# Masked scores set to one value in the heads by queries, no mean of v put in, POOL and two-input DVE work planned as one resource, identity products in PE's gaps

## The chip, the cores and the metric

The kernel runs on one core of one Trainium2 chip. Its engines work side by side, each through its own list of instructions in order: TensorE (PE, with its weight loads PEld), VectorE (DVE), ScalarE (ACT), GpSimd (POOL) and SyncE (SP, which only issues transfers). The metric is the device time of one execution in microseconds: the median of three is 716.46 (716.38 to 717.63).

## The reference

Two parts follow each other: attention in which a query sees only the keys of its own hash bucket, then an MLP with a gate that mixes over the sequence.

```python
batch, n_heads, seq, head_dim = (4, 8, 768, 64)      # proj: (64, 6); d_model 512, d_ff 1024
def _attn_ref(q, k, v, proj):
    scale = 1.0 / np.sqrt(D)
    q_bits = (np.einsum('bhsd,dk->bhsk', q, proj) > 0).astype(np.int64)
    k_bits = (np.einsum('bhsd,dk->bhsk', k, proj) > 0).astype(np.int64)
    q_bucket = np.sum(q_bits * powers, axis=-1)
    k_bucket = np.sum(k_bits * powers, axis=-1)
    mask = q_bucket[:, :, :, None] == k_bucket[:, :, None, :]
    scores = scale * np.matmul(q, k.transpose(0, 1, 3, 2))
    scores = np.where(mask, scores, -1000000000.0)
    scores = scores - np.max(scores, axis=-1, keepdims=True)
    attn = np.exp(scores)
    attn = attn / (np.sum(attn, axis=-1, keepdims=True) + 1e-09)
    return np.matmul(attn, v).astype(np.float32)
def _moe_ref(x, w_in, w_spatial, b_spatial, w_out):
    h = np.maximum(x @ w_in, 0.0)
    u, v = (h[..., :d_ff // 2], h[..., d_ff // 2:])
    v_n = (v - mean(v)) / np.sqrt(var(v) + 1e-06)
    v_s = np.einsum('ts,bsd->btd', w_spatial, v_n) + b_spatial[None, :, None]
    return ((u * v_s) @ w_out).astype(np.float32)
```

A query whose bucket holds no key has all its scores at the same value after the mask. Its softmax is even over the 768 keys, and its output is the mean of v over the sequence.

## The kernel before, in words

**Tiles and loops.** The 32 heads of the four batches are taken two at a time: 16 pairs, four to a batch. A pair is worked through in 6 steps of 128 rows, so there are 96 steps. Numbers are kept to about the precision of float32 by splitting each one into two float16 parts, a high one and the rest; hence the many operations named `high` and `low`, and the three products for each product of the reference.

**The mask.** `hash_rows` takes the signs of the projections, and writes them by DMA (L367) as extra rows beside the rows of q and k. One more product over these rows adds a large negative number to every score whose buckets differ, larger with each bit in which they differ. So masked scores are far below the others, yet not all alike.

**Heads by queries and heads by keys.** Most heads are worked by queries (`by_queries`): a tile has 128 queries by 768 keys. DVE reads the scores from PSUM, scales them and takes the minimum of their negatives along the row (L486, which writes `ex` and the row's number into `nb`); ACT makes the exponential with `nb` as its bias (L489) and the high half (L493); DVE or POOL makes the rest (L497); SP issues a transposing DMA, `pt` from `pp` (L501); and PE multiplies by v (`weighted`, L607). The heads in the set `WIDE`, 2, 4 and 6, are worked by keys (`by_keys`): a tile has 128 keys by 768 queries, in float32, with no transpose. Their row maximum must be known beforehand: `row_max` computes the scores another time on PE, DVE reduces them (L554), and `max_row` turns the result and moves it by DMA (L581) into one of the mask's rows. All scores of the pair wait for that row.

**The mean of v.** A row without a key has masked scores that differ among themselves, so its softmax isn't even. For each pair `mean_v` (POOL, L417, L421, L424) and `mean_row` (PE L437, ACT L441) compute the mean of v. For each head `normalize` multiplies the result of such rows by zero (the third small DVE operation of `factor`, L632), makes a tile with the mean in these rows and zero elsewhere (`none`, POOL, L624 and L625) and adds it (`add`, POOL, L639; DVE for the last head). Then come the split of x (ACT L646, DVE L649) and its transpose.

**The MLP of a batch** is cut into units of PE work (`v_unit`, `u_unit`, `s_unit`, `o_unit`; PE line L702 for all). Their rank comes after that of the scores, so they fill what PE leaves free in the attention of the next batch. `norm` has the layer norm: statistics on DVE, the inverse root by ACT and a small Newton step, scaling on DVE (L834), the high part on ACT (L839), the rest on POOL (L843). In `s_unit` two products of 128x384 (L903, L906) are on POOL, in the last batch on DVE or POOL. The weights come as 64-bit or 32-bit numbers, and 24 of the 36 jobs in `weights` are converted by four DVE instructions (L287 to L292), two or three of ACT and one of POOL (L303).

**What sets the order.** A planner, run when the program is built. Every operation is an `Op` with its engine (or two to choose from, as "VG" for DVE or POOL), an assumed duration, what it depends on, the buffers it holds, and a rank. `timetable` plays the engines forward: the engine that can start first takes the ready operation of the lowest rank; PSUM banks of two pools, `m` and `pv`, are counted. The sequence of planned starts is then each engine's real order. At run time only the data dependences hold an engine back; the planned times themselves don't. The scores of step g are not planned before a time that grows by `T_FIRST`, `T_KEYS`, `T_QUERIES` or `T_LAST` a step, and the weights' jobs not before `W_FROM - 6 + W_EVERY * i`. DVE and POOL are planned as though they never met.

## Time and profile before

| | us |
|---|---|
| median of 3 executions | 716.46 (716.38 to 717.63) |
| the profiled execution | 722.25, its span 720.5 |
| PE busy | 632.9 (88%), mean granted clock 0.94 |
| DVE busy | 550.1 (76%) |
| ACT busy | 463.1 (64%) |
| POOL busy | 427.0 (59%) |
| transposing DMAs `pt` from `pp` | 174 |
| heads by queries, by keys | 29, 3 |

The span is the time from the first to the last instruction of the one profiled execution, which is a little longer than the others. A group's row gives its busy time, the mean length of one instruction in ns, and after the bar the idle time of the engine just before these instructions, with what ended it. The length of an instruction includes time in which it has been started and can't go on. The chain of waits is followed back from the last instruction: at each step to what released it.

### The profile page before, as it was taken

The numbers are of one execution on the slowest core, as the hardware profiler recorded it, in microseconds if no ns is written. First come the engines' busy times: TensorE is split into PE (matmuls) and PEld (weight loads), VectorE is DVE, ScalarE is ACT, GpSimd is POOL, SyncE is SP. The second block draws the span as 40 slices with busy tenths as digits, with TensorE's granted clock in tenths as the row PEclk, the third lists the DMA queues.
The fourth block names the chain that finished last, engine by engine and source line by source line (L and its number), as shares of the span: only waits on it lengthen the run. The fifth ranks groups of instructions, "written<-read, shape, count | busy, mean of one in ns | idle before, by whom it ended". The sixth has DMA issues, their size and how long they took to land.

```text
span 720.5 us, 16877 instructions
## 1 busy us (share of the span) xinstructions
PE 632.9 (88%) x6667; PEld 371.5 (52%) x6667; DVE 550.1 (76%) x1004; ACT 463.1 (64%) x707; POOL 427.0 (59%) x456
## 2 busy tenths in 40 slices
PE   3778989876887899789999899879899999989997
PEld 1344757643544555446544565445454556545553
DVE  6997977979799989687878997967879794273250
ACT  2956665978786777667686677666677784443112
POOL 6581853688556788967857686856867545025000
PEclk9876988988999999899999899989999999999999
DMA  5896876699999699999999799899788998000102
GB/s 184 183 216 137 137 173 145 132 200 203 198 209 187 116 185 186 220 190 226 185 179 203 140 172 211 165 158 199 158 162 133 210 136 137 0 15 30 45 1 87
DMA packets 318259, 110.84 MB, mean 154 GB/s; under 512 B 305124, under 2 KB 308196, under 8 KB 318180
## 3 DMA queue, kind: packets, MB, share of 16 engines
q1 hardware_dynamic: 314244, 108.62, 77.4%
q0 software_dynamic: 3840, 1.12, 1.0%
q8 instruction: 52, 0.85, 0.5%
q14 instruction: 27, 0.22, 0.1%
q10 hardware_dynamic: 96, 0.04, 0.0%
HBM read 27.94 MB, written 6.29 MB: 48 GB/s over the span
## 4 chain that ended last, share of the span: by engine, by line
PE 35%; DVE 28%; DMA 13%; ACT 11%; issue 9%; POOL 2%; SPq 0%; DVEq 0%; ACTq 0%; POOLq 0%
DMA pt<-pp 10%; DVE ex L486 9%; PE sps L702 8%; PE sp L459 7%; PE ops L702 6%; PE pv L607 6%; DVE pp L497 5%; ACT pp L493 4%; ACT ex L489 3%; DVE hl L385 3%; PE ups L702 3%; PE vpp L702 2%; PE mx L459 2%; DVE vr L834 1%; DVE bs L791 1%
## 5 line engine op out<-in xcount | busy, mean ns | idle before, releaser
L489 ACT ACTIVATE ex<-ex,nb 128x768 f32<-128x768 f32 x174 | 157.9, 933 | 94.7 <-DVE ex L486 94.6
L497 POOL TENSOR_TENSOR pp<-ex,pp 128x768 f16<-128x768 f32 x76 | 136.1, 1792 | 93.2 <-ACT pp L493 85.5
L486 DVE TENSOR_SCALAR_CACHE_REDUCE ex<-sp 128x768 f32<-128x768 f32 x174 | 160.0, 949 | 22.0 <-PE sp L459 21.9
L497 DVE TENSOR_TENSOR pp<-ex,pp 128x768 f16<-128x768 f32 x98 | 123.8, 1266 | 44.8 <-ACT pp L493 43.3
L607 PEld LDWEIGHTS <-pt 128*128 128x128 f16 x3132 | 116.5, 100 | 61.4 <-issue 34.3
L459 PE MATMUL sp<-hl 64*128 64x384 f16 x1080 | 124.5, 351 | 25.4 <-DVE ex L486 23.8
L493 ACT CAST pp<-ex 128x768 f16<-128x768 f32 x174 | 138.5, 822 | 7.2 <-DMA pt<-pp 6.6
L607 PE MATMUL pv<-vp,pt 128*128 128x65 f16 (+1 forms) x3132 | 128.5, 197 | 16.5 <-DVE x L636 9.2
L702 PE MATMUL sps<-ws,vn 128*128 128x384 f16 x576 | 101.1, 326 | 2.1 <-ACT vr L785 2.0
L459 PEld LDWEIGHTS <-hl 64*128 64x128 f16 x1104 | 56.8, 100 | 88.6 <-issue 64.2
L702 PEld LDWEIGHTS <-vn 128*128 128x128 f16 x576 | 53.8, 98 | 36.6 <-issue 3.8
L702 PE MATMUL ops<-wo,g 128*128 128x512 f16 x288 | 67.5, 382 | 3.2 <-DVE u L865 3.2
L702 PE MATMUL ups<-xt,wi 128*128 128x384 f16 x348 | 66.2, 334 | 2.9 <-DVE sg L352 2.8
L367 POOL DMA_DIRECT2D hk<-sg x112 | 59.5, 537 | 14.7 <-PE pv L607 6.8
L459 PE MATMUL sp<-hk 63*128 63x384 f16 (+1 forms) x360 | 54.7, 348 | 8.4 <-DMA hk<-sg 5.9
L702 PE MATMUL vps<-wi,xt 128*128 128x512 f16 x234 | 56.5, 379 | 1.7 <-ACT vr L785 1.2
L903 POOL TENSOR_TENSOR sy<-sy,u 128x384 f32<-128x384 f32 x24 | 27.2, 1134 | 49.3 <-DVE sy L891 48.9
L702 PEld LDWEIGHTS <-wi 128*128 128x128 f16 x384 | 35.8, 100 | 27.2 <-issue 6.2
L891 DVE SCALAR_TENSOR_TENSOR sy<-sps,bt 128x384 f32<-128x384 f32 x32 | 17.7, 552 | 36.2 <-PE sps L702 36.1
L702 PEld LDWEIGHTS <-g 128*128 128x128 f16 x288 | 26.7, 98 | 34.1 <-issue 5.8
L639 POOL TENSOR_TENSOR x<-x,xf 128x384 f32<-128x384 f32 x31 | 34.6, 1115 | 11.1 <-DVE x L636 8.7
L702 PEld LDWEIGHTS <-xt 128*128 128x128 f16 x288 | 25.9, 97 | 29.1 <-issue 3.7
(111 smaller groups left out, 845.7 us busy)
## 6 DMA issues: line engine op xcount, KB each, us to landing
qk<-kq SPq DMA_DIRECT2D x16, 768.0 KB
out<-o SPq DMA_DIRECT2D x24, 256.0 KB
v<-v SPq DMA_DIRECT2D x13, 384.0 KB
pt<-pp SPq DMA_TRANSPOSE x174
raw<-w_in SPq DMA_DIRECT2D x8, 256.0 KB
raws<-w_in SPq DMA_DIRECT2D x8, 256.0 KB
hk<-sg POOLq DMA_DIRECT2D x112, 9.0 KB, 3.5
vf<-v SPq DMA_DIRECT2D x3, 384.0 KB
```

Source lines behind the costliest of these rows:

```text
L367: eng.dma_start(out=hkt(p)[D * e:D * e + 2 * NB, 1 - j // 2, (j % 2) * HS:(j % 2 + 1) * HS], in_=sg[1][32 * j + 16 * e:32 * j + 16 * e + 2 ...
L385: op("V", 0.9, lambda to=to, part=part, frm=frm: nc.vector.scalar_tensor_tensor(out=st["hl", p][:, to], in0=st["qk", p][:, part], scalar=S ...
L459: nc.tensor.matmul(ps[e][:, c - halves[0]], lhsT=src[r, l, rows], rhs=src[r, m, cs], start=(a == 0), stop=(a == len(passes) - 1))
L486: nc.vector.tensor_scalar(ex, st["sc", p, i][e], -ISQ, None, op0=ALU.mult, op1=ALU.min, accum_out=st["nb", n][:, i:i + 1])
L489: nc.scalar.activation(st["e32", n, i], st["e32", n, i], AF.Exp, bias=st["nb", n][:, i:i + 1], scale=-1.0)
L493: nc.scalar.copy(st["pp", n, i][:, 0], st["e32", n, i])
L497: eng.tensor_tensor(out=st["pp", n, i][:, 1], in0=st.pop(("e32", n, i)), in1=st["pp", n, i][:, 0], op=ALU.subtract)
L607: nc.tensor.matmul(o, lhsT=l, rhs=m, start=(i == 0 and k == 0), stop=(i == NT - 1 and k == len(todo_) - 1))
L639: eng.tensor_add(st["x", n], st["x", n], st["f"])
L702: nc.tensor.matmul(c[0], lhsT=l(), rhs=r(), start=(j == 0), stop=(j == len(products) - 1))
L891: nc.vector.scalar_tensor_tensor(out=y[0], in0=c[0], scalar=1.0 / (SN * SW), in1=bt[:, hs], op0=ALU.mult, op1=ALU.add)
L903: t1 = op(*POST[last], lambda: either(t1).tensor_mul(y[0], y[0], u[h][:, d]), t, done["u", d, h], on=[hy, hu[h]], rank=2)
```

## The change

In heads by queries the DVE pass over the scores becomes a maximum with -2^28, a number between the real and the masked scores: all masked scores of a tile take that one value, and the row's maximum comes out beside them. A new small operation, `bias`, on ACT or POOL by the plan, multiplies the maximum by a constant for the exponential's bias, and the exponential has the scale. A row without a key has then 768 equal scores. So these heads need no mean of v, no `none`, no `add` and no third operation in `factor`; the heads by keys still do.

Head 2 goes from the heads by keys to the heads by queries. The planner marks the operations of POOL (but not its DMA issues, nor `bias`) and most of DVE's operations with two SBUF inputs or of the small `tensor_scalar` kind as `alone`: one of them is not planned before the one before it has ended. Several assumed durations are changed to go with it. The layer norm's scaling moves from DVE to ACT, with one more small DVE operation for its bias. The two products in `s_unit` may be on DVE in every batch, and the `low` of `normalize` on POOL. Wherever the plan has PE idle for over 0.5 us after its first 5 us and a bank of `m` is free, `warm` puts products of the identity with itself there, one for each 0.08 us. The steps of heads by queries are planned 6.0 us apart, not 5.8, and the weights' jobs 2.6 us apart, not 3.6.

```diff
-    WIDE = {2, 4, 6}
+    WIDE = {4, 6}
 def op(..., alone=False):
+        o.need, o.gives, o.alone = need, gives, alone or "G" in e and fn.__name__ not in ("move", "bias")
 timetable:
+        port = [0.0]
+        fill = []
             if not o.need:
-                return o.ready
+                return max(o.ready, port[0]) if o.alone else o.ready
...
+            gap = t - free[e]
+            if e == "P" and gap > GAP and free[e] > WARM and banks["m"] and min(banks["m"]) < free[e]:
+                fill.append((free[e], int((gap - 0.1) / 0.08)))
...
+            if o.alone:
+                port[0] = end
...
+        for t, n in fill:
+            op("P", 0.0, lambda n=n: warm(n)).start = t
+
+    def warm(n):
+        b = bank_m("warm")
+        for _ in range(n):
+            nc.tensor.matmul(b[:, :P], lhsT=ident, rhs=ident, start=True, stop=True)
 mean_v, mean_row:
+        if not keys(p):
+            return
 by_queries:
-            nc.vector.tensor_scalar(ex, st["sc", p, i][e], -ISQ, None, op0=ALU.mult, op1=ALU.min, accum_out=st["nb", n][:, i:i + 1])
+            nc.vector.tensor_scalar(ex, st["sc", p, i][e], -float(2 ** 28), None, op0=ALU.max, op1=ALU.max, accum_out=st["mx", n][:, i:i + 1])
+        def bias():
+            nb, mx = st["nb", n][:, i:i + 1], st["mx", n][:, i:i + 1]
+            if t1.e == "G":
+                nc.gpsimd.tensor_scalar(nb, mx, -ISQ, None, op0=ALU.mult)
+            else:
+                nc.scalar.activation(nb, mx, AF.Copy, scale=-ISQ)
-            nc.scalar.activation(st["e32", n, i], st["e32", n, i], AF.Exp, bias=st["nb", n][:, i:i + 1], scale=-1.0)
+            nc.scalar.activation(st["e32", n, i], st["e32", n, i], AF.Exp, bias=st["nb", n][:, i:i + 1], scale=ISQ)
...
-        t = t3 = op("VG", (1.1, 1.75), rest, t, on=[hx, hp], rank=(g, 1 + e))
+        at["nb", n] = t = t1 = op("AG", BIAS, bias, t, on=[held["nb", n], held["mr", n]], rank=(g, 0.1 + 0.1 * e))
+        t = t3 = op("VG", REST, rest, t, on=[hx, hp], rank=(g, 1 + e))
 normalize:
-            nc.vector.scalar_tensor_tensor(out=rv, in0=st["nb", n], scalar=ISQ * 2 ** 28, in1=rv, op0=ALU.is_le, op1=ALU.mult)
+            if n in KEYS:
+                nc.vector.scalar_tensor_tensor(out=rv, in0=st["nb", n], scalar=ISQ * 2 ** 28, in1=rv, op0=ALU.is_le, op1=ALU.mult)
-        at["xs", n] = op("V", 0.5, low, t, on=[hx, hs], rank=(g, 0.8))
+        at["xs", n] = op("VG", (0.55, 1.0), low, t, on=[hx, hs], rank=(g, 0.8))
 s_unit, norm:
-    POST = {False: ("G", 1.15), True: ("VG", (0.5, 1.15))}
+    POST = ("VG", (0.56, 1.0))
+                nc.vector.scalar_tensor_tensor(out=ve, in0=mv[g][:, :, 0], scalar=-1.0, in1=r, op0=ALU.mult, op1=ALU.mult)
-                    nc.vector.tensor_scalar(v32[i], v32[i], mv[g][:, j, 0:1], c["r"][:, j:j + 1], op0=ALU.subtract, op1=ALU.mult)
+                    nc.scalar.activation(v32[i], v32[i], AF.Identity, bias=c["ve"][:, j:j + 1], scale=c["r"][:, j:j + 1])
 constants:
-    T_FIRST, T_KEYS, T_QUERIES, T_LAST = 5.0, 4.8, 5.8, 5.8
+    T_FIRST, T_KEYS, T_QUERIES, T_LAST = 5.0, 4.8, 6.0, 6.0
+    REST, BIAS = (0.96, 1.68), (0.25, 0.25)
+    GAP, WARM = 0.5, 5.0
-    W_FROM, W_EVERY = 20.0, 3.6
+    W_FROM, W_EVERY = 20.0, 2.6
```

More of the change, by code (lines that the diff above doesn't have):

```diff
@@ L82, in __init__ @@
             self.left, self.then, self.ready, self.start = 0, [], 0.0, None
-            self.need, self.gives = None, None
+            self.need, self.gives, self.alone = None, None, None
             ops.append(self)
@@ L101, in __init__, with op @@
             self.users, self.before, self.closed = [], [], False
-    def op(e, d, fn, *after, on=(), rank=4, land=0.0, dma=0.0, need=None, gives=None):
+    def op(e, d, fn, *after, on=(), rank=4, land=0.0, dma=0.0, need=None, gives=None, alone=False):
         o = Op(e, d, fn, rank, land, dma)
-        o.need, o.gives = need, gives
+        o.need, o.gives, o.alone = need, gives, alone or "G" in e and fn.__name__ not in ("move", "bias")
         wait = [a for a in after if a is not None]
@@ L211, in lsh_attention_spatial_gating @@
     nc.sync.dma_start(out=hc, in_=hconst)
+    make_identity(nc, ident)
     ws = [const.tile([P, NT, S], F16, name=f"ws{i}") for i in range(2)]
@@ L232, in lsh_attention_spatial_gating @@
     nc.gpsimd.memset(ones, 1.0)
-    make_identity(nc, ident)
     wi = [const.tile([P, NPAIR, DF], F16, name=f"wi{i}") for i in range(2)]
@@ L407, in split_v @@
         t = op("A", 0.15 + 0.6 * z, high, at["v", p], *after, on=[held["v", p], h], rank=(NT * p - 1, 4))
-        at["vp", p] = op("V", 0.1 + 0.8 * z, low, t, on=[held["v", p], h], rank=(NT * p - 1, 4))
+        at["vp", p] = op("V", 0.1 + 0.8 * z, low, t, on=[held["v", p], h], rank=(NT * p - 1, 4), alone=True)
     def mean_v(p, *after):
+        if not keys(p):
+            return
         va, vc = buf("pf", 1).new(), buf("vc", 1).new()
@@ L424, in three @@
             nc.gpsimd.tensor_add(st["vc", p], st["vc", p], st["va"][:, 4:6])
-        t = op("G", 1.05, one, at["v", p], *after, on=[held["v", p], va])
-        t = op("G", 0.5, two, t, on=[va, vc])
-        at["vc", p] = op("G", 0.5, three, t, on=[va, vc])
+        t = op("G", 0.95, one, at["v", p], *after, on=[held["v", p], va])
+        t = op("G", 0.45, two, t, on=[va, vc])
+        at["vc", p] = op("G", 0.45, three, t, on=[va, vc])
     def mean_row(p, *after):
+        if not keys(p):
+            return
         vc, fm = held["vc", p], buf("fm", 2).new()
@@ L554, in high @@
                 nc.vector.reduce_max(st["mx", 2 * p + e][:, i, c:c + 1], ps[e], axis=AX.XY)
-            at["mx", 2 * p + e] = op("V", 0.5, high, t, on=[held["mx", 2 * p + e]], rank=R_MAX, gives="m")
+            at["mx", 2 * p + e] = op("V", 0.55, high, t, on=[held["mx", 2 * p + e]], rank=R_MAX, gives="m")
     def max_row(p):
@@ L613, in normalize @@
         p, e = divmod(n, 2)
-        end = n == 2 * NP - 1
-        hf, hr, hx = buf("pf", 1).new(), buf("rv", 2).new(), buf("x", 2).new()
+        hf, hr, hx = buf("pf", 1).new() if n in KEYS else None, buf("rv", 2).new(), buf("x", 2).new()
         if e == 0:
@@ L960, in lsh_attention_spatial_gating @@
     mean_v(0)
-    maxima = [(max(NT * (n // 2) + i - 7, 1 + i // 2), n // 2, i) for n in sorted(KEYS) for i in range(NT)]
+    maxima = [(max(NT * (n // 2) + i - 7, 1 + i // 2, NT * (n // 2 - 1) + 1 + i // 2 if n > 7 else 0), n // 2, i) for n in sorted(KEYS) for i in range(NT)]
     lag = [LAGK if n in KEYS else LAG0 if n < 2 * NPAIR else LAG for n in range(2 * NP)]
```

64 lines of the change are left out of this document (33 added, 31 removed).

## The prediction

> **What bounds the kernel now.** I read the page first: busy shares, traffic by slice, chain of waits.
>
> ```profile
> PE 632.9 (88%) x6667; PEld 371.5 (52%) x6667; DVE 550.1 (76%) x1004; ACT 463.1 (64%) x707; POOL 427.0 (59%) x456
> ```
> ```profile
> GB/s 184 183 216 137 137 173 145 132 200 203 198 209 187 116 185 186 220 190 226 185 179 203 140 172 211 165 158 199 158 162 133 210 136 137 0 15 30 45 1 87
> ```
> ```profile
> PE 35%; DVE 28%; DMA 13%; ACT 11%; issue 9%; POOL 2%; SPq 0%; DVEq 0%; ACTq 0%; POOLq 0%
> DMA pt<-pp 10%; DVE ex L486 9%; PE sps L702 8%; PE sp L459 7%; PE ops L702 6%; PE pv L607 6%; DVE pp L497 5%; ACT pp L493 4%; ACT ex L489 3%; DVE hl L385 3%; PE ups L702 3%; PE vpp L702 2%; PE mx L459 2%; DVE vr L834 1%; DVE bs L791 1%
> ```
>
> No engine owns the chain. PE has the largest share, DVE the next. The chain uses 28% of the span in DVE work while DVE is busy 76% of it: 28/76 = 0.37 of a microsecond of DVE work lies on the chain. For ACT it is 11/64 = 0.17. These two ratios turn work into time below; they are my choice, and blunt.
>
> Then I cut the span in three, at the first scores of batch 1 and after the last scores (the instructions of L486 and L522 in order of time), and asked for the busy time of each engine in each stretch. Columns: stretch, its length, busy us with instructions for PE, PEld, DVE, ACT and POOL, granted clock, DMA share, GB/s.
>
> ```profile
> 0.00:155.40 155.40, 123.28 (x1233) 78.44 (x1233) 127.41 (x253) 102.89 (x162) 94.34 (x119) 0.86 0.79 166
> 155.40:604.00 448.60, 400.63 (x4784) 233.71 (x4777) 380.64 (x669) 325.90 (x479) 313.03 (x318) 0.95 0.97 180
> 604.00:720.50 116.50, 108.97 (x664) 59.34 (x660) 42.10 (x85) 34.28 (x66) 19.60 (x20) 1.00 0.12 37
> ```
>
> Stage 1 is batch 0, with no MLP to fill PE and a low clock. Stage 2 is batches 1 to 3 with the MLP of the batch before. The tail is PE alone. In stage 2 DVE is busy 85%, but not all of that is work. The timeline of POOL, then of DVE, at one place (start, us, engine, line, operation, tiles):
>
> ```profile
> 464.40 1.02 POOL L903 TENSOR_TENSOR sy<-sy,u 128x384 f32<-128x384 f32 x1
> 465.37 1.78 POOL L906 TENSOR_TENSOR g<-sy,g 128x384 f16<-128x384 f32 x2
> 467.11 0.99 POOL L639 TENSOR_TENSOR x<-x,xf 128x384 f32<-128x384 f32 x1
> 468.07 0.97 POOL L624 TENSOR_SCALAR fl<-nb 128x6 f32<-128x6 f32 x1
> ```
> ```profile
> 464.59 5.23 DVE L497 TENSOR_TENSOR pp<-ex,pp 128x768 f16<-128x768 f32 x2
> ```
>
> The first of the two DVE subtractions stands through four POOL instructions on end, the last of them L639, and the 6-column L624 in turn lasts 0.97. By line, with minimum/median/maximum in ns:
>
> ```profile
> L497 DVE TENSOR_TENSOR pp<-ex,pp x98: 941/959/4360, 22.0 to 603.2; 128x768 f16<-128x768 f32 x98
> ```
> ```profile
> L649 DVE TENSOR_TENSOR xs<-x,xs x32: 544/559/1941, 74.4 to 615.5; 128x384 f16<-128x384 f32 x32
> ```
> ```profile
> L834 DVE TENSOR_SCALAR vr<-vr,mv,rs x24: 533/540/1933, 237.0 to 644.7; 128x512 f32<-128x512 f32 x24
> ```
> ```profile
> L624 POOL TENSOR_SCALAR fl<-nb x32: 218/230/967, 52.7 to 612.5; 128x6 f32<-128x6 f32 x32
> ```
> ```profile
> L486 DVE TENSOR_SCALAR_CACHE_REDUCE ex<-sp x174: 923/948/959, 18.5 to 599.4; 128x768 f32<-128x768 f32 x174
> ```
>
> L486, which reads PSUM, never stretches; two-input operations and L834 do, to four times. So POOL and these DVE operations exclude one another, and DVE loses to a train of POOL work.
>
> **The change part by part.** Groups by line: busy us, mean ns | idle before.
>
> ```profile
> L497 POOL TENSOR_TENSOR pp<-ex,pp 128x768 f16<-128x768 f32 x76 | 136.1, 1792 | 93.2 <-ACT pp L493 85.5 <-DMA pt<-pp 2.8 <-issue 2.3
> L497 DVE TENSOR_TENSOR pp<-ex,pp 128x768 f16<-128x768 f32 x98 | 123.8, 1266 | 44.8 <-ACT pp L493 43.3 <-DMA v<-v 0.5 <-DMA pt<-pp 0.3
> L639 POOL TENSOR_TENSOR x<-x,xf 128x384 f32<-128x384 f32 x31 | 34.6, 1115 | 11.1 <-DVE x L636 8.7 <-DMA pt<-pp 1.5
> L625 POOL TENSOR_TENSOR xf<-fm,fl 128x384 f32<-128x384 f32 x32 | 29.6, 926 | 2.7
> L649 DVE TENSOR_TENSOR xs<-x,xs 128x384 f16<-128x384 f32 x32 | 25.8, 816 | 3.3 <-ACT xs L646 3.2
> L554 DVE TENSOR_REDUCE mx<-mx 128x1 f32<-128x384 f32 x36 | 19.0, 550 | 1.5 <-PE mx L459 1.1
> L834 DVE TENSOR_SCALAR vr<-vr,mv,rs 128x512 f32<-128x512 f32 x24 | 16.1, 716 | 0.1
> L624 POOL TENSOR_SCALAR fl<-nb 128x6 f32<-128x6 f32 x32 | 14.5, 453 | 3.2 <-DVE ex L486 3.2
> L417 POOL TENSOR_TENSOR va<-v 128x384 f32<-128x384 f32 x13 | 14.1, 1081 | 5.3 <-DMA v<-v 5.2
> L839 ACT CAST vn<-vr 128x512 f16<-128x512 f32 x24 | 13.7, 615 | 4.6 <-DVE vr L834 4.0 <-PE sps L702 0.5
> L424 POOL TENSOR_TENSOR vc<-vc,va 128x128 f32<-128x128 f32 x16 | 10.9, 683 | 1.1
> L421 POOL TENSOR_TENSOR vc<-va 128x128 f32<-128x128 f32 x16 | 10.2, 637 | 0.8
> L632 DVE SCALAR_TENSOR_TENSOR rv<-nb,rv 128x6 f32<-128x6 f32 x32 | 9.3, 292 | 1.1
> L437 PE MATMUL mp<-vc,ones 128*128 128x128 f32 x32 | 8.5, 351 | 6.4 <-POOL vc L424 3.0 <-POOL xf L625 2.0 <-DVE mt L578 0.5
> L441 ACT ACTIVATE fm<-mp 128x128 f32<-128x128 f32 x16 | 4.3, 271 | 13.1 <-PE mp L437 13.1
> L817 ACT ACTIVATE rs<-ve 128x3 f32<-128x3 f32 x8 | 1.6, 200 | 2.5 <-DVE ve L813 2.5
> L206 ACT ACT_TABLE_LOAD x1 | 1.3, 1283 | 0.7 <-PEq L1062 0.7
> ```
>
> *The mean of v.* 30 of 32 heads lose L624 and L625, (14.5 + 29.6) x 30/32 = 41 us of POOL; L639 stays for 2 of its 31, 34.6 x 29/31 = 32; L417, L421 and L424 stay for 2 pairs of 16, 35.2 x 14/16 = 31. POOL gives up 104 of 427 us. POOL is only 2% of the chain, 14 us, so directly this is 14 x 104/427 = 3, put at 4 with the wait for L639. PE loses 8.5 x 14/16 = 7 us and ACT (L441) 4, 5 and 3 of them in stage 2; with 35/88 = 0.4 of PE's work on the chain that is - 2. The rest of the worth is the exclusion. The fillers' identity is made earlier on POOL, at the start, where POOL has only constants to write: nothing, or half a microsecond if the hash rows of pair 1 were late for it.
>
> *The exclusion.* Busy less count times median: L497 123.8 - 94.0 = 30, L649 25.8 - 17.9 = 8, L834 16.1 - 13.0 = 3: 41 us of DVE standing (other two-input lines come on top, uncounted), some 31 in stage 2 and 10 before. It falls with POOL's cut alone by a quarter, and the plan now keeps both out of each other's way; but no wait between the engines enforces that. I take two thirds (bounds: one quarter, all): 21 and 7 us of DVE, on the chain 21 x 0.37 = 8 and 2.5.
>
> *DVE work that goes from stage 2.* L834 to ACT: 16.1 - 3.1 already counted = 13, three quarters here, 10. L632 for 30 heads, three quarters: 7. The weights come every 2.6 instead of 3.6 us of the plan, and their conversion leaves this stage:
>
> ```profile
> 155.40:604.00 448.60, 4.46 (x8) 0.95 0.97 180
> ```
>
> That is L287, the first of four DVE instructions of a job: 8 of 24 jobs, some 15 us in all four (estimate: 4.46 x 3.5). They land in stage 1 at + 15 x 0.37 = 5.5. Stage 2: (10 + 7 + 15) x 0.37 = 12 less. L649 may now go to POOL and the MLP's two products to DVE; these moves oppose each other and I put them at zero, with 32 x 0.559 = 18 us of DVE as bound.
>
> *Added.* 180 bias operations of one column (29 + 1 heads by 6), on ACT or POOL by the plan: nearest rows L817, 200 ns, and L624, 230 ns when unhindered. Half on ACT is 72 in stage 2, 14 us; L834's successor on ACT like L839, 18 x 0.615 = 11. ACT + 25, less the 3, x 0.17 = 4 us more. Its cover is ACT's idle time, 448.6 - 325.9 = 123; without it, 25. The new function of that operation could bring table loads; bounds 0 and 24 loads (L206, 31 us of ACT, 5 on the chain), and I take 0, as the present kernel changes among five functions with one load.
>
> *Head 2 by queries.* Its row maximum goes, and with it the row that the scores of pair 1 wait for. PE's timeline:
>
> ```profile
> 41.29 1.81 PE L607 MATMUL pv<-vp,pt 128*128 128x65 f16 x54
> 47.32 1.42 PE L459 MATMUL mx<-ws 64*128 64x384 f16 x4 [4.22 <-DVE mx L554]
> ```
> ```profile
> 57.66 2.10 PE L459 MATMUL sp<-ws 64*128 64x384 f16 x12
> ```
> ```profile
> 60.79 0.82 PE L459 MATMUL sp<-ws 64*128 64x384 f16 x4 [1.03 <-DMA ws<-mt]
> ```
>
> From 41.3 to 60.8 PE makes maxima between idle times and no scores; a step of stage 1 takes some 155/24 = 6.5. So 19.5 - 6.5 = 13, of which I take 12. In its place come 6 steps with L486 at 0.95, a split and a transpose each (6 more on SP's queue, one row less); the 12 maxima it loses were 12 x 0.55 = 6.6 us of DVE (L554), the six L486 are 5.7 and the subtractions come on top, so + 1.
>
> *Fillers.* The plan puts identity products into gaps over 0.5 us. Price of one from the last transposes:
>
> ```profile
> 616.26 0.50 PE L672 MATMUL xp<-ident,xs 128*128 128x128 f16 x6
> ```
>
> 6 in 0.50, so under 83 ns each, about the 80 that the plan assumes. They stand in idle time where the plan is right. Worth: with the clock at 0.86 and 0.95, at most 0.14 x 123 = 17 us in stage 1 and 0.05 x 401 = 20 in stage 2; at the other end they push late work back by as much. I take - 3 and - 2. The Trainium skill, "TensorE: Matmul & The Clock Gate", section on the HAM clock gate, says that the clock falls after an idle window of some 3.4 us; by that, filling gaps of half a microsecond keeps nothing warm, and these 5 us would be 0.
>
> *Sum.* Stage 1: - 12 + 1 - 2.5 + 5.5 - 3 = - 11. Stage 2: - 4 - 2 - 8 - 12 + 4 - 2 = - 24. Tail: the last head's addition goes, from DVE under PE's work, for nothing; some MLP that stage 2 no longer has room for, + 2. Together - 33: the profiled execution, 722.25 with the 1.75 around its span of 720.5, becomes 689. It lies 5.8 above the median 716.46; the median becomes **683**.
>
> **The rivals.**
>
> *PE carries the work over* (704). PE is at 89% in stage 2; if its share stays, 24 us less of stage is 24 x 0.89 = 21 us of MLP moved to a tail that is 94% PE: + 23. Left are - 11 and - 1. For: the tail is all PE. Against: much of PE's idle time waits on the chain that shortens.
>
> *More than the chain says* (664). DVE in stage 2 loses 21 + 32 of 381 us; if the stage follows DVE in proportion, 448.6 x 53/381 = 62 less, capped by PE: 401 x 0.95 = 381 of warm work at a 95% share is 401, so - 48. With - 11 of stage 1 and 7 carried over, 716 - 52. DMA allows it: it moves 226 GB/s in one slice against 180 on average.
>
> *The bias delays ACT* (726, the slower side). The exponential stands behind the bias in ACT's order. On POOL the bias is behind subtractions and the exclusion, which the plan doesn't charge it with: L624, just as small, takes 453 ns on average against 230. Behind half of an L497 on POOL (1792 ns) too, the delay is 1.1 us; with all 144 of stage 2 there, 160 us, against ACT's idle 123 less the 11 of the scaling. The excess is 48: 716.46 - 11 - 24 + 48 = 729, and 726 when a few go to ACT. It decides from a mean delay of (112 + 35)/144 = 1.0 us. Against: the plan sees POOL's queue and gives the bias to whoever is free.
> The Trainium skill, "SBUF — State Buffer", section "Who interferes with whom", says that a GpSimd operation and a two-input DVE operation block each other for the whole instruction; the trace agrees by the 0.97 us above, and by that rule the uncharged bias is the weak place of this plan.
>
> *The plan doesn't hold on the chip.* Only a quarter of the standing goes: 10 x 0.37 = 4 instead of 10.5, so 690; inside the forecast's own range.
>
> **How the numbers follow.** Forecast 683 with its neighbours: 0.50. More than the chain: 0.22. Carried over: 0.15. Bias or fillers delaying: 0.10. No change, the gains eaten: 0.03. I call 0.2% (1.4 us) what can be told from no change. Faster: 0.50 + 0.22 + 0.15 = 0.87; slower 0.10; same 0.03. Range: low end 655, nine under the larger gain, for the bounds of exclusion and clock; high end 712, beyond the carried-over case, without the slower one.
>
> **What would show it.** Right: POOL some 60 to 100 us less busy, L497 on DVE near 1.0 us mean, no 20 us without scores near 45, last scores near 570, tail near 116 to 120. Wrong: L497 still above 1.2 us, ACT idle behind the bias, a tail over 130, or fillers standing in front of scores that are ready.

## The result: 706.67 us, a third of the gain forecast

The changed kernel takes 706.67 us in the median of four executions (703.99 to 709.59), the kernel before beside it 717.05. The ratio is 0.985 (95% interval 0.9812 to 0.9888), so it is faster by 1.5%, some 10 us, where 33 were forecast. The number is close to that of the rival "PE carries the work over" (704), but not by that rival's way, as shown below.

The page of the changed kernel: busy shares, then the chain of waits by engine and by line.

```profile
PE 634.7 (90%) x7475; PEld 394.9 (56%) x7475; DVE 519.7 (74%) x997; ACT 502.4 (72%) x822; POOL 271.5 (39%) x368
...
PE 43%; ACT 19%; DMA 16%; DVE 9%; issue 8%; POOL 2%; SPq 2%; DVEq 0%; ACTq 0%; POOLq 0%
DMA pt<-pp 12%; PE sps L734 11%; ACT ex L519 7%; PE sp L480 7%; PE pv L637 7%; PE ops L734 7%; ACT pp L523 6%; DVE ex L509 5%; PE vps L734 4%; PE ups L734 3%; DVE pp L527 2%; PE vpp L734 2%; SPq L531 1%; POOL pp L527 1%; DMA raws<-w_sp 1%
```

DVE went from 28% of the chain to 9%, POOL from 427 us busy to 272. PE and ACT took most of DVE's place, and the transposes went from 10% to 12%. In the same three stages (length, busy us of PE, PEld, DVE, ACT, POOL, clock, DMA share, GB/s):

```profile
0.00:139.90 139.90, 115.61 (x1582) 83.08 (x1583) 110.39 (x222) 100.87 (x166) 77.09 (x103) 0.96 0.95 189
139.90:583.50 443.60, 404.73 (x5179) 248.11 (x5177) 365.52 (x686) 362.99 (x585) 191.69 (x263) 0.98 1.02 186
583.50:702.20 118.70, 114.39 (x720) 63.74 (x718) 43.77 (x92) 38.52 (x72) 2.74 (x3) 1.00 0.12 36
```

Batch 0 is 15.5 us shorter, batches 1 to 3 only 5.0, the tail 2.2 longer. (The two profiled executions differ by 18 us, more than the medians: 703.99 is the shortest of its four.) The gain that failed to come is that of batches 1 to 3: 24 forecast. What PE does of the MLP, batch by batch (stretch, length, busy us with products of PE and weight loads, clock, DMA), before and after:

```profile
155.40:306.30 150.90, 50.24 (x243) 22.28 (x243) 0.93 0.99 188
306.30:453.70 147.40, 74.41 (x357) 31.81 (x357) 0.97 1.00 188
453.70:604.00 150.30, 74.86 (x357) 31.77 (x357) 0.97 0.90 164
604.00:720.50 116.50, 106.60 (x580) 56.37 (x579) 1.00 0.12 37
```
```profile
139.90:292.50 152.60, 36.62 (x174) 16.54 (x174) 0.97 1.07 199
292.50:441.40 148.90, 76.12 (x365) 32.83 (x366) 0.99 1.01 183
441.40:583.50 142.10, 79.25 (x403) 36.64 (x402) 1.00 0.98 176
583.50:702.20 118.70, 109.61 (x598) 57.94 (x596) 1.00 0.12 36
```

The MLP is the same work in all, about 300 us of PE. In batch 1 PE now does 174 of its products instead of 243, in a stretch no shorter. The products not done there are done later, and the tail stays. By line, the last conversion of the weights (POOL, `wo`) and the first gate product (`sps`), before and after, with ns minimum/median/maximum and the first and last start:

```profile
L303 POOL TENSOR_TENSOR wo<-w,wo x8: 659/1144/1427, 175.9 to 234.7; 128x256 f16<-128x256 f32 x8
```
```profile
L702 PE MATMUL sps<-ws,vn x576: 322/326/505, 257.3 to 700.9; 128*128 128x384 f16 x192
```
```profile
L320 POOL TENSOR_TENSOR wo<-w,wo x8: 658/675/1402, 193.2 to 261.7; 128x256 f16<-128x256 f32 x8
```
```profile
L734 PE MATMUL sps<-ws,vn x576: 322/326/525, 287.0 to 683.1; 128*128 128x384 f16 x192
```

Batch 0 ends 15 us sooner, yet the weights are ready 27 us later and the gate starts 30 us later. The weight jobs are read into the tiles `g` and `u` that the MLP of batch 0 needs, so the plan puts half of `ups` and all of `sps` behind the last job. I call this theory W. PE's products of the MLP around this moment, before and after (start, us, engine, line, operation, tiles):

```profile
256.30 0.65 PE L702 MATMUL ups<-xt,wi 128*128 128x384 f16 x3
257.34 1.62 PE L702 MATMUL sps<-ws,vn 128*128 128x384 f16 x9
```
```profile
224.07 0.65 PE L734 MATMUL ups<-xt,wi 128*128 128x384 f16 x3
263.03 1.14 PE L734 MATMUL ups<-xt,wi 128*128 128x384 f16 x6
287.03 1.14 PE L734 MATMUL sps<-ws,vn 128*128 128x384 f16 x6
```

In the kernel before the gate follows `ups` at once; its MLP has no pause over 7 us on PE from 177 to 288. In the changed kernel PE has no product of the MLP from 224.7 to 263.0, and the second half of `ups` comes as the last conversion ends. The gate comes 24 us after that, with the last part of `vn`, the output of the layer norm:

```profile
257.81 0.42 DVE L309 SCALAR_TENSOR_TENSOR w<-raws,w 128x256 uint32<-128x256 uint32 x1
259.21 0.23 DVE L845 TENSOR_SCALAR ve<-mv 128x3 f32<-128x3 f32 x2
286.64 1.22 POOL L876 TENSOR_TENSOR vn<-vr,vn 128x512 f16<-128x512 f32 x1 [0.61 <-ACT vn L872]
```

The layer norm's small steps on DVE (L845) start just behind the last DVE step of the weights (L309), and the plan ranks them after the weights. So what the gate waits for last is the layer norm, and the late weights seem to hold it up too; that the rank is the reason is argued, not tested. (In k4, below, these steps come at 210, long before the last conversion, and there the gate waits for the weights alone.) The rivals in the expectations are A (ACT has become the bound), T (the transposes) and F (the fillers).

### The profile page after: what moved, and what is told of

Its sections match the earlier page's. It is cut to its first block, busy times and chain, and to the rows that moved or that the text cites. A ratio compares the mean times of both kernels' runs of the same rounds, so it can differ in the third digit from the quotient of the medians.

```text
span 702.2 us, 18439 instructions
## 1 busy us (share of the span) xinstructions
PE 634.7 (90%) x7475; PEld 394.9 (56%) x7475; DVE 519.7 (74%) x997; ACT 502.4 (72%) x822; POOL 271.5 (39%) x368
## 4 chain that ended last, share of the span: by engine, by line
PE 43%; ACT 19%; DMA 16%; DVE 9%; issue 8%; POOL 2%; SPq 2%; DVEq 0%; ACTq 0%; POOLq 0%
DMA pt<-pp 12%; PE sps L734 11%; ACT ex L519 7%; PE sp L480 7%; PE pv L637 7%; PE ops L734 7%; ACT pp L523 6%; DVE ex L509 5%; PE vps L734 4%; PE ups L734 3%; DVE pp L527 2%; PE vpp L734 2%; SPq L531 1%; POOL pp L527 1%; DMA raws<-w_sp 1%
## 5 line engine op out<-in xcount | busy, mean ns | idle before, releaser
L527 DVE TENSOR_TENSOR pp<-ex,pp 128x768 f16<-128x768 f32 x133 | 139.1, 1064 | 61.2 <-ACT pp L523 60.5
L519 ACT ACTIVATE ex<-ex,nb 128x768 f32<-128x768 f32 x180 | 167.5, 934 | 22.4 <-POOL nb L514 18.2
L637 PE MATMUL pv<-vp,pt 128*128 128x65 f16 x3240 | 126.3, 194 | 26.3 <-DMA pt<-pp 24.2
L480 PE MATMUL sp<-hl 64*128 64x384 f16 x1080 | 109.6, 328 | 13.8 <-DVE ex L509 13.0
L527 POOL TENSOR_TENSOR pp<-ex,pp 128x768 f16<-128x768 f32 x47 | 77.5, 1655 | 39.6 <-ACT pp L523 32.8
L514 POOL TENSOR_SCALAR nb<-mr 128x1 f32<-128x1 f32 x81 | 24.4, 301 | 142.7 <-DVE ex L509 115.7
L208 PE MATMUL warm<-ident 128*128 128x128 f16 x825 | 56.0, 224 | 0.0
L208 PEld LDWEIGHTS <-ident 128*128 128x128 f16 x825 | 48.7, 100 | 9.8 <-issue 9.3
L516 ACT ACTIVATE nb<-mr 128x1 f32<-128x1 f32 x99 | 19.4, 196 | 48.2 <-DVE ex L509 48.1
L932 ACT CAST g<-sy 128x384 f16<-128x384 f32 x32 | 16.2, 508 | 41.4 <-DVE sy L936 41.1
```

The lines of the kernel that those rows point to most:

```text
L208: nc.tensor.matmul(b[:, :P], lhsT=ident, rhs=ident, start=True, stop=True)
L480: nc.tensor.matmul(ps[e][:, c - halves[0]], lhsT=src[r, l, rows], rhs=src[r, m, cs], start=(a == 0), stop=(a == len(passes) - 1))
L514: nc.gpsimd.tensor_scalar(nb, mx, -ISQ, None, op0=ALU.mult)
L516: nc.scalar.activation(nb, mx, AF.Copy, scale=-ISQ)
L519: nc.scalar.activation(st["e32", n, i], st["e32", n, i], AF.Exp, bias=st["nb", n][:, i:i + 1], scale=ISQ)
L527: eng.tensor_tensor(out=st["pp", n, i][:, 1], in0=st.pop(("e32", n, i)), in1=st["pp", n, i][:, 0], op=ALU.subtract)
```

## The experiments

Each was timed beside the kernel before on the same chip; the ratio is to that one. The changed kernel's own is 0.985. "Kept" means that every engine's order is that of the parent; otherwise the planner made a new one.

| run | parent | order | us | ratio (95%) |
|---|---|---|---|---|
| e1 no fillers | after | kept | 702.2 | 0.9759 (0.9728 to 0.9791) |
| e2 weights without DVE | after | new | 686.6 | 0.9537 (0.9496 to 0.9577) |
| e3 half the transposes | after | kept | 686.8 | 0.9534 (0.9491 to 0.9576) |
| e4 no bias | after | kept | 691.5 | 0.9618 (0.9583 to 0.9652) |
| f1 bias on ACT | after | kept | 703.2 | 0.9777 (0.9728 to 0.9826) |
| k1 scaling on DVE | after | kept | 707.8 | 0.9857 (0.9797 to 0.9916) |
| g1 scaling on DVE | after | new | 694.8 | 0.9655 (0.9634 to 0.9675) |
| f2 no common resource | after | new | 703.9 | 0.9795 (0.975 to 0.984) |
| f3 head 2 by keys | after | new | 700.9 | 0.9773 (0.9727 to 0.982) |
| g4 no freedom | after | new | 737.3 | 1.0239 (1.0208 to 1.0269) |
| k4 other order | after | new | 711.0 | 0.9895 (0.9846 to 0.9944) |
| f4 one value only | before | new | 716.1 | 0.9979 (0.9956 to 1.0002) |
| k3 freedom only | before | new | 735.8 | 1.0245 (1.0186 to 1.0304) |
| h1 weights without DVE | before | new | 706.7 | 0.9835 (0.9803 to 0.9866) |
| n1 half the transposes | before | kept | 707.0 | 0.9852 (0.9781 to 0.9923) |
| g3 own tiles for weights | after | new | 686.9 | 0.954 (0.9517 to 0.9564) |
| n2 own tiles, other order | after | new | 697.9 | 0.9712 (0.9649 to 0.9775) |
| k2 own tiles, scaling on DVE, two constants | after | new | 687.6 | 0.9573 (0.9521 to 0.9624) |

**How much an order does by itself (k4).**

```diff
-    START = 9.0
+    START = 9.05
```

> The changed kernel with the first scores planned 0.05 us later (START 9.05 instead of 9.0): the same operations in an order made anew, to show what an order alone does. If the verdicts on kernels with a new order are to stand to some 5 us: 702 to 712. If more: outside.

Measured 711.0 for the same operations, planned 0.05 us later: 4 us more than the changed kernel, with intervals that overlap. Inside, much more moves: the last conversion starts at 291.8 instead of 261.7, and PE does 126 products of the MLP in batch 1 instead of 174. So a difference of a few us between kernels of new orders says nothing, and g1 and k1 below suggest that it can be 12.

**The weights (e2, h1).** The edit leaves out the four DVE instructions of each of 24 jobs, in the plan too, so those weights are not the reference's.

```diff
-                t = op("V", 0.28, lambda c=c: nc.vector.tensor_scalar(c["w"], c["w"], TINY, ...
-                t = op("V", 0.25, ...
-                t = op("V", 0.45, ...
-                t = op("V", 0.45, ...
```

> The changed kernel without the four DVE instructions of each of the 24 weight jobs (the numbers in those weights are left wrong), so DVE has 34 us less and the weights are ready sooner. Theory W: the last weights at about 190 us instead of 262, the first gate products (sps) by 230 instead of 287, and 680 to 690 in all. Theories A (ACT with its bias and scaling is the new bound) and T (the transposes are): DVE is not the bound in either, so 700 to 706.

> The kernel before (717) without the four DVE instructions of the weight jobs (numbers in those weights left wrong). The same edit took 20 us from the changed kernel. If the kernel before starves PE in batch 1 in the same way (sps at 257 us, last weights at 235): 694 to 703. If the gate is new with the change: 708 to 717.

Measured 686.6, 20 us less than the changed kernel. Rows of e2: the weights, the gate, and the MLP in batch 1 and in the tail.

```profile
L313 POOL TENSOR_TENSOR wo<-w,wo x8: 671/676/1237, 156.9 to 196.5; 128x256 f16<-128x256 f32 x8
```
```profile
L727 PE MATMUL sps<-ws,vn x576: 323/326/337, 238.7 to 667.1; 128*128 128x384 f16 x192
```
```profile
146.10:296.20 150.10, 62.37 (x309) 27.54 (x309) 0.99 1.04 190
...
587.40:686.20 98.80, 92.00 (x500) 48.47 (x498) 1.00 0.12 39
```

The attention is no faster: batches 1 to 3 begin at 146, 296 and 444 (139.9, 292.5 and 441.4 in the changed kernel). But PE does 309 MLP products in batch 1 instead of 174, and the tail is 20 us shorter, 98.8 instead of 118.7. So the gain came as theory W has it: PE did earlier what it had been kept from. With e2 alone one can't part this from DVE's 34 us less work and a new order; g3 below keeps that work.

In the kernel before the same edit gives 12 us (h1: 706.7, between the two ranges expected), and by another way. Its gate moves from 257 to 245.5 only, PE does 258 products in batch 1 instead of 243, and the tail stays; but the last pass over scores starts at 583.7 instead of 599.4 (the spans of the two profiled executions are 17.5 us apart). There the weights' work on DVE cost the attention some time. The pause in PE's MLP is new with the change.

**The weights' tiles (g3, n2).** The remedy: late jobs are read into two tiles of their own, `sps` waits for `w_sp` alone, no fillers.

```diff
-        RB = [i % 4 if i < MANY else i % 2 for i in range(36)]
+        RB = [i % 4 if i < MANY else 4 + i % 2 for i in range(36)]
+                if RB[i] > 3:
+                    t = wk.tile([P, 4 * 256], F16, tag=f"rw{RB[i]}", name=f"raw{i}")
-... [done["vn", i] for i in range(NT)] + at["ws"] + at["wo"], bank(), [hy, hg[h]])
+... [done["vn", i] for i in range(NT)] + at["ws"], bank(), [hy, hg[h]])
-    EB, PB, PTB, XTB, VB, UB = 4, 4, 9, 6, 6, 2
+    EB, PB, PTB, XTB, VB, UB = 4, 4, 9, 5, 6, 2
-    MANY = 36
+    MANY = 21
```

> The changed kernel without fillers; the weight jobs from the 22nd on are read into two tiles of their own instead of tiles that the MLP of batch 0 needs (one buffer of xt given up for the space), and the gate product waits for w_sp alone, not for w_out. Theory W: the gate product starts by 240 instead of 287, the tail gets shorter by some 12 us, and 685 to 695. If W were not the cause: 700 to 706, as without fillers (702).

> The version with tiles of their own for the late weight jobs (686.9), now from the 21st job on instead of the 22nd, so the same remedy in another order. An order alone moved the changed kernel by 4 us (k4). If the remedy and not a lucky order gave the 20 us: 684 to 694. If it was the order: 695 to 705.

g3 took 686.9, 4.6% less than the kernel before and the fastest version that computes the whole. Its rows for the last conversion and the first gate product:

```profile
L320 POOL TENSOR_TENSOR wo<-w,wo x8: 668/676/1439, 186.7 to 257.8; 128x256 f16<-128x256 f32 x8
```
```profile
L734 PE MATMUL sps<-ws,vn x576: 323/326/337, 259.3 to 666.5; 128*128 128x384 f16 x192
```

`wo` is nearly as late as in the changed kernel, but the gate no longer waits for it: it starts at 259 instead of 287 (240 was expected). n2 has the same remedy from the 21st job on, and took 697.9. That lies in the range that was expected if g3's gain was its order. Beside the changed kernel without fillers, 702, the remedy gave 15 us in g3 and 4 in n2, and the interval of n2 overlaps that of e1. n2's gate starts early too, at 265.6. So the traces of e2, g3 and n2 show that the gate can come earlier; g3 shows that this can be worth time, and the size stays open.

**The transposes (e3, n1).** Half the bytes in each transpose; the order kept.

```diff
-            nc.sync.dma_start_transpose(out=st["pt", n, i], in_=st.pop(("pp", n, i)).rearrange("p g c k -> p (g c k)"))
+            nc.sync.dma_start_transpose(out=st["pt", n, i][:, 0:NT], in_=st.pop(("pp", n, i))[:, 1].rearrange("p c k -> p (c k)"))
```

> The changed kernel with each transpose of a head by queries moving only the second half of pp (768 of 1536 columns), used for both halves in the product with v; the rest adds instead of subtracting, so that sums stay above zero. Instructions keep their order. Theory T (transposes, 0.95 to 1.02 of the 16 DMA engines): PE's wait for them, 24 us in pv and 35 in weight loads, goes, and 680 to 692. Theory W: those waits were filled or made up later, 699 to 706. Theory A: 702 to 707.

> The kernel before (717) with each transpose of a head by queries moving only the second half of pp, used for both halves in the product with v; the rest adds instead of subtracting; order kept. The same edit took 20 us from the changed kernel. If transposes bound the kernel before as much: 695 to 701. If they became a bound only when DVE and POOL were relieved, as the forecast's sum supposed them hidden: 710 to 717.

e3 gave 20 us, n1 11. What PE and its weight loads wait for a transposed tile, in the kernel before, the changed one and e3 (us in total, times, longest):

```profile
PEld L607 <- DMA pt<-pp: 16.8, 24, 1.7
PE pv L607 <- DMA pt<-pp: 5.7, 10, 1.0
```
```profile
PEld L637 <- DMA pt<-pp: 35.4, 37, 3.0
PE pv L637 <- DMA pt<-pp: 24.2, 22, 2.7
```
```profile
PEld L637 <- DMA pt<-pp: 3.5, 4, 1.4
PE pv L637 <- DMA pt<-pp: 2.5, 3, 1.2
```

PE and its weight loads wait for transposes in the kernel before, 22.5 us in these rows, and more in the changed one, 59.6 us. n1 lies between its two ranges: the transposes already cost the kernel before something. Theory T holds beside theory W: e3 does no more of the MLP in batch 1, but its batches are 145, 144 and 142 us long instead of 153, 149 and 142.

**The bias (e4, f1).** First no bias at all, then all 180 on ACT; the order kept in both.

```diff
         def bias():
-            nb, mx = ...
+            pass
-            nc.scalar.activation(..., AF.Exp, bias=st["nb", n][:, i:i + 1], scale=ISQ)
+            nc.scalar.activation(..., AF.Exp, scale=ISQ)
```
```diff
-            if t1.e == "G":
+            if False:
```

> The changed kernel without the 180 bias operations (99 on ACT, 19 us; 81 on POOL, 24 us): the exponential has no bias and follows DVE's maximum directly; order kept. Theory A: ACT is 19% of the chain, and 19 us of work and 18 us of waiting for POOL go; 685 to 695. Theory W: 701 to 706, as ACT's work ends earlier and PE doesn't.

> The changed kernel (706.7) with all 180 bias operations on ACT, none on POOL; planned order kept. If the 15 us that leaving the bias out saved are the hop through POOL (18 us of ACT waiting for it, 301 ns mean there), 695 to 702. If they are ACT's load, 16 us more of ACT work: 709 to 718. If either place costs the same: 703 to 709.

Without it 691.5, 15 us less, in the range of theory A. With all of it on ACT 703.2, whose interval overlaps that of the changed kernel: the place hardly matters, and 16 us more of work on ACT didn't show. In the changed kernel the two forms are:

```profile
L514 POOL TENSOR_SCALAR nb<-mr 128x1 f32<-128x1 f32 x81 | 24.4, 301 | 142.7 <-DVE ex L509 115.7
```
```profile
L516 ACT ACTIVATE nb<-mr 128x1 f32<-128x1 f32 x99 | 19.4, 196 | 48.2 <-DVE ex L509 48.1
```

44 us of small operations cost 15 us: one more step between DVE's maximum and the exponential. Which share is the step and which is ACT's time stays open.

**The fillers (e1).**

```diff
-        for t, n in fill:
-            op("P", 0.0, lambda n=n: warm(n)).start = t
```

> The changed kernel (706.7) without the 825 identity products; all other instructions keep their order. Theory W (in batch 1 PE starves until the last weights are converted at 262 us, and what it doesn't do there comes back in the tail): the fillers stand in idle time, so 704 to 712; the clock in batch 0 falls from 0.96 to about 0.87 and costs up to 8 us there. Theory F (fillers stand in front of ready work, 56 us of PE): 680 to 695.

702.2, and the intervals of the two ratios don't meet: the fillers cost 0.9%, some 6 us, though the mean clock is 0.966 to 0.983 in the four executions with them and 0.946 to 0.953 in the four without. Neither theory had that. Batch 1 begins at 140.5 without them and 139.9 with them, so they bought next to nothing in batch 0. One place where they cost can be read: in the tail, where PE is the bound. The fillers' busy time in the tail of the changed kernel, and e1's tail:

```profile
583.50:702.20 118.70, 3.45 (x56) 1.00 0.12 36
```
```profile
584.00:700.70 116.70, 111.40 (x664) 60.57 (x662) 43.32 (x92) 38.46 (x72) 2.74 (x3) 1.00 0.12 37
```

56 identity products lie there at a clock that is full without them, and the tail is 2.0 us shorter when they go.

**The layer norm's scaling (g1, k1).** On DVE again, with a new order and with the old one. The second edit is this line alone:

```diff
-                    nc.scalar.activation(v32[i], v32[i], AF.Identity, bias=c["ve"][:, j:j + 1], scale=c["r"][:, j:j + 1])
+                    nc.vector.tensor_scalar(v32[i], v32[i], mv[g][:, j, 0:1], c["r"][:, j:j + 1], op0=ALU.subtract, op1=ALU.mult)
```

> The changed kernel (706.7) with the layer norm's scaling on DVE again and without the small operation for its bias; order made anew. If ACT is one of the bounds of batches 1 and 2, 15 us less on it in all: 696 to 703. If DVE's 13 us more weigh as much: 704 to 710.

> The changed kernel (706.7) with the layer norm's 24 scalings issued on DVE instead of ACT, every operation kept at its place in the plan (the small operation for the bias stays). If the 12 us that this move gave with an order made anew are ACT's load in batches 1 and 2: 694 to 700. If they were mostly the new order: 703 to 709.

g1 took 694.8, just under its ranges, as if the move to ACT had cost 12 us. k1 took 707.8: with the order kept the move is worth nothing that can be measured (its interval is some 4 us to each side). So g1's gain comes with its order. And k2, which puts g3's remedy and this one together (with the planner's look-ahead `LOOK` at 0 instead of 0.2 and the remedy from the 23rd job on, so it is not g3 with one thing more),

> Both remedies together: the late weight jobs in tiles of their own (686.9 alone), scaling on DVE (694.8 alone), no fillers, order made anew. If the two causes are separate: 672 to 680. If the earlier MLP and the freed ACT buy the same PE time: 683 to 690.

took 687.6, no better than g3 alone.

**The parts of the change (f4, f2, f3, k3, g4).** f4 is the kernel before with the first part only. f2 and f3 undo one part of the changed kernel. g4 takes from it, and k3 gives to the kernel before, the freedom to put the MLP's two products and the low half in `normalize` on either engine.

```diff
f2:
-        o.need, o.gives, o.alone = need, gives, alone or "G" in e and fn.__name__ not in ("move", "bias")
+        o.need, o.gives, o.alone = need, gives, False
f3:
-    WIDE = {4, 6}
+    WIDE = {2, 4, 6}
g4 (k3 the other way round):
-    POST = ("VG", (0.56, 1.0))
+    POST = ("G", 1.0)
-        at["xs", n] = op("VG", (0.55, 1.0), low, t, on=[hx, hs], rank=(g, 0.8))
+        at["xs", n] = op("V", 0.55, low, t, on=[hx, hs], rank=(g, 0.8))
```

> The kernel before (717) with only the first part of the change: masked scores set to one value, bias operations, no mean of v for heads by queries; head 2 by keys, old durations, no common resource, no fillers, scaling on DVE. If leaving the mean of v out carries the gain: 700 to 710. If the bias takes most of it back, as 15 us against POOL's 104 us less: 710 to 717. Batch 1's MLP starts no sooner, so not below 700.

> The changed kernel with the planner not treating POOL and two-input DVE work as one resource (nothing is marked alone); its order is made anew. If that planning is what won: L527 on DVE above 1.2 us mean again and 712 to 725. If the exclusion no longer matters with POOL at 39%: 700 to 710. A new order alone may move the time by some 5 us.

> The changed kernel with head 2 by keys again (row maximum and the row that pair 1 waits for), order made anew. The forecast gave head 2 by queries 11 us in batch 0: then batch 1 begins near 150 instead of 140, and 706 to 717, the less the more of it is lost before the weights are ready. Theory W, by which batch 0 isn't what sets the end: 702 to 708 with batch 1 beginning later all the same.

> The changed kernel with the MLP's two products on POOL alone and the low half in normalize on DVE alone, as before; order made anew. The first part of the change by itself gave 716, the whole 707. If the freedom to put these operations on either engine carries the difference: 714 to 735. If not: 702 to 710.

> The kernel before (717) with only the freedom: the MLP's two products in every batch, and the low half in normalize, on DVE or POOL by the plan. Taking this freedom from the changed kernel cost 30 us. If it is worth much alone: 700 to 710. If only together with POOL's relief and the common resource: 712 to 722.

f4 gained nothing that can be measured, 0.9979 with 1 inside its interval, though POOL has 81 us less to do (its page):

```profile
PE 622.3 (87%) x6641; PEld 366.5 (51%) x6641; DVE 519.5 (73%) x969; ACT 483.7 (68%) x805; POOL 346.1 (49%) x399
```

That is the range expected if the bias, which f4 adds, takes back what POOL's relief gives; f4 doesn't part the two. Its stages, batches 1 to 3 and the tail, are:

```profile
150.50:586.40 435.90, 386.89 (x4735) 224.81 (x4732) 353.71 (x645) 342.00 (x555) 248.75 (x277) 0.96 1.00 185
586.40:712.40 126.00, 118.81 (x686) 64.26 (x682) 42.29 (x82) 37.42 (x72) 21.51 (x20) 0.98 0.13 35
```

Batches 1 to 3 are 12.7 us shorter than in the kernel before and the tail 9.5 longer (the two spans are 8.1 us apart). Here the rival "PE carries the work over" can be seen.

f2 and f3 are not slower than the changed kernel (700.9 for f3, under both its ranges), so neither part carries the gain by itself as far as runs with new orders can tell. But f2's equal time hides two large moves: the last conversion, the MLP in batch 1 and the tail are

```profile
L320 POOL TENSOR_TENSOR wo<-w,wo x8: 664/674/1390, 195.7 to 234.8; 128x256 f16<-128x256 f32 x8
```
```profile
154.10:308.40 154.30, 52.74 (x261) 23.54 (x261) 0.99 1.00 187
607.00:703.90 96.90, 90.05 (x491) 47.57 (x489) 1.00 0.13 42
```

Without the common resource batch 1 begins at 154.1, 14 us later; the weights are ready 27 us earlier, as in the kernel before, though they keep the new constant of 2.6; and the tail is 22 us shorter. The four DVE instructions of each job are among those marked `alone`. In the five traces without the common resource that keep these instructions (the kernel before, n1, f4, k3, f2; four orders) the last conversion starts between 225 and 242, in all thirteen with it (eight orders) between 252 and 292. So the weights come late with the common resource. It seems to be what shortens batch 0 too.

The subtraction on DVE in the changed kernel and in f2:

```profile
L527 DVE TENSOR_TENSOR pp<-ex,pp 128x768 f16<-128x768 f32 x133 | 139.1, 1064 | 61.2 <-ACT pp L523 60.5
```
```profile
L527 DVE TENSOR_TENSOR pp<-ex,pp 128x768 f16<-128x768 f32 x106 | 125.7, 1188 | 80.2 <-ACT pp L523 79.5
```

The plan does what it says: an instruction stands 0.11 us on average over its median of 0.96 with it, 0.23 without it, and 0.31 in the kernel before. The time doesn't follow.

The freedom is worth 30 us in the changed kernel (g4: 737) and costs 17 to 18 in the kernel before (k3: 736); both lie above their ranges. Both went through new orders, but these are beyond what an order did in k4 and g1. In g4 the whole loss lies in the tail, which is 31 us longer:

```profile
585.70:735.70 150.00, 135.80 (x733) 70.98 (x731) 1.00 0.12 35
```

Its gate starts at 313.5 and PE does 120 products of the MLP in batch 1. In k3 it is batches 1 and 2 that are longer, 156 us each instead of 151 and 147. I read it as the freedom helping only a plan whose other costs fit it; that reading is argued, not shown. Which part of the change won the 10 us stays open.

## Why the prediction was wrong

**The direction was right, and the number for batch 0 near.** 15.5 us in the profiles against 11. But the step that was to win them, head 2, isn't shown to have done it: f3 has the row maximum back, and its batch 1 begins at 136.5. The fillers didn't (140.5 without them). Only f2, without the common resource, begins as late as 154.1. So the number for batch 0 owes much to luck. The term for head 2 was also misread: the row at 57.66 is 12 score products of pair 1, so PE was without scores for 16 us, not 19.5, and only the next four waited for the row, 1.0 us.

**The step that failed: what leaves batches 1 to 3.** The forecast took 24 us from them, and 5.0 came. Half of the 24 was work that leaves DVE there, and a third was less standing. The terms were wrong as follows.

**The weights.** The prediction read "every 2.6 instead of 3.6 us of the plan" as earlier conversions, took 15 us of DVE out of batches 1 to 3 and 6 us of time with it. The opposite came: 12 of the 24 first DVE steps of the jobs (L304) lie in batches 1 to 3, not 8.

```profile
139.90:583.50 443.60, 3.56 (x12) 0.98 1.02 186
```

Four of the 12 come before 156 us, about where batch 0 used to end; what is really later is the last eight. The constant only says when a job may start: the last from 140 us on before and from 105 now, long before it does. f2 points to the common resource for the rest, and the prediction gave that resource credit for less standing and no price. Nor did the prediction see what waits behind the weights, half of `ups` and all of `sps`. Letting the gate go earlier was worth 15 us in g3 and 4, not clear of noise, in n2.

**DVE's relief was sized wrongly.** Forecast: 53 us less DVE in batches 1 to 3. The stage shows 381 before and 366 now. The standing went as forecast: busy less count times median is 139.1 - 133 x 0.958 = 12 us for the subtraction, 30 before, where two thirds were to go. But 133 subtractions are now on DVE, not 98: 35 more, 34 us: 29 came over from POOL and 6 are those of head 2. The diff lowers the assumed duration on DVE from 1.1 to 0.96, but f2 has that too and keeps 106 on DVE; so most of this move, like the weights', comes with the common resource. With these subtractions and others POOL lost 156 us, not 104. The prediction weighed the other moves between the two engines and not this one.

**The exchange rate.** It priced a microsecond of DVE at 0.37 on the chain. By that rate the 15 us that DVE did lose there are 5.6 us, near the 5.0 measured; one such agreement proves little. Against the rate speaks f2, which doubles the standing per instruction and isn't slower, though its order is new. When DVE gave way, DMA, ACT and PE were right behind: 16%, 19% and 43% of the chain. The transposes had no term in the sum. They were worth 11 us in the kernel before and 20 in the changed one. "DMA allows it", from the fastest slice of 226 GB/s, read a mean where a wait decides.

**A term that was left out.** The steps of heads by queries are planned 6.0 us apart instead of 5.8: 0.2 us for each of the 72 steps of batches 1 to 3 are 14 us, if the engines' order carries the spacing into the run. The sum puts it at nothing without a word. No run changes it alone, so what it cost stays open.

**The bias** was a term of + 4 us and measured 15. The rival in which it makes the kernel slower did not come: POOL's 301 ns on average, and ACT waited 18 us in all for it, 0.2 us for each of the 81, far under the mean of 1.0 us from which it would decide. f1 gives no sign that POOL's queue is the cost.

**The fillers** were to give 5 us and cost 6. The clock did rise, from 0.95 to between 0.966 and 0.983; that was not worth what it cost.

**The scaling's move to ACT** was priced within + 4 us of ACT, with some 2 us; k1 finds nothing, but can't see 2 us. So the term failed by the bias.

**The carried work.** The rival said 704, and that its number is near is luck. By its mechanism batches 1 to 3 get 24 us shorter and the tail 23 longer; they got 5.0 shorter and the tail 2.2 longer. Part of it holds: PE does the same 300 us of MLP, and what doesn't happen in batch 1 comes later. But the reason is another: not that PE was already full, but that for 38 us it had no product of the MLP that it was allowed to do.

## What to carry to other kernels

Where one engine's total sets the end and low-ranked work is to fill its gaps, ask first when that work becomes available and what it waits for: relief of the other engines before that moment is lost, as it was in batch 1. Read a planner's constant together with the ranks, buffers and resources that can overrule it. When a diff binds work to a common resource, ask what has to give way: here it was the weights. When a change seems to do nothing, compare the stages: in f2 two moves of 14 and 22 us cancel. Before one part of a replanned kernel is credited with a few us, rerun it with the order kept where it can be: 12 us of g1 vanished in k1.

## What the runs showed of the hardware that was not expected

A higher granted clock is not the same as less time: 0.966 to 0.983 with 825 identity products against 0.946 to 0.953 without them, and 0.9% slower. The DMA share of a stage can't be read as use of a fixed whole: it stands above 1, 1.02 in batches 1 to 3 of the changed kernel and 1.07 in its batch 1; halving the transposes' bytes took it to 0.66 and the time down by 20 us. And single-column operations cost about 0.2 us each on POOL and ACT alike (208 and 198 ns in the median), yet leaving 180 of them out of a chain gave 15 us.
